# Moving twenty reciprocals of an RWKV-7 / gated-MLP kernel from the vector engine to powers on GpSimd

## The chip, the cores and the metric

The kernel runs on one core of a Trainium2 chip. A core has five engines that each work through their own instruction queue in order: TensorE (PE, matrix products and transposes, with a separate row PEld for its weight loads), VectorE (DVE), ScalarE (ACT), GpSimd (POOL) and SyncE (SP), which here only issues DMAs. The engines wait for each other through semaphores. The metric is the device time of one execution in microseconds. The kernel before has a median of 783.92 us (two runs, 782.73 and 785.11).

## The reference

Two computations follow each other, all in float32. The first is a recurrence over 768 steps for 4 batches times 8 heads with a 40x40 state each, the second a feed-forward block over the 3072 resulting tokens:

```python
for t in range(S):                                   # S = 768, state is D x D, D = 40
    y[:, :, t] = einsum('bhd,bhde->bhe', rt, state)
    Sa = einsum('bhde,bhe->bhd', state, at)
    state_decay = state * wt[:, :, None, :] - einsum('bhd,bhe->bhde', Sa, bt)
    state = state_decay + einsum('bhd,bhe->bhde', vt, kt)
x = y.transpose(0, 2, 1, 3).reshape(B * S, H * D)    # 3072 x 320
h = x @ w_in                                         # 320 x 2048
out = (h * cos(h)) @ w_out                           # 2048 x 320
```

The decay `w` lies between 0.85 and 0.95. The MLP weights arrive as float64.

## The kernel before, in words

The recurrence is cut into **24 units** (`NU`): a unit is a chunk of 64 time steps (`C`) of two of the four batches, all eight heads, laid out as 128 partitions (2 batches x 64 steps) by 8 x 40 elements. Units 2c and 2c+1 hold the two batch pairs of chunk c. Within a chunk the running product W of the decays is needed, because the chunk form of the recurrence works with a·W, b/W and k/W. For units 0 to 3 the running product is scanned on DVE and transposed back through PSUM (`wn`); from unit 4 on it is computed earlier for a whole quarter of the sequence (`ws_scan`, `ws_join`, `ws_down`, `ws_store`), written to DRAM (`wd`), and loaded into the buffer `nat["w", u]`, in SBUF. "The decay" below is this running product.

`over_w(u, wn)` makes `rw` = 1/W (128x320) with one `nc.vector.reciprocal` (L399) and `bn` = b·rw on GpSimd (L400). `p2_kn` (L653) later makes `kn` = k·rw on GpSimd and copies v (L654). The consumers are these: `p1_b` ("pb") turns the `bn` of two units on PE (L364, tile `bT`), `p1_n` ("pn") multiplies bT with aT, and a triangular system per unit is inverted on DVE in many small steps (`inv_step`, `pair_step`, L530 and L534: a multiplication and a subtraction with both inputs in SBUF). `p2_k` turns `kn` (tile `kT`), `p2_g`, `ch_t`, `ch_q`, `ch_ag`, `ch_xa`, `ch_s`, `ch_z` are the chain of matrix products that carries the state from unit u to unit u+2. In `ch_z` GpSimd multiplies the new state by the last decay (`qz`, L802) and the output by W (`yt`, L817), after DVE has added them up (L801, L812). `tokens` and `back` send `yt` through DRAM to make the tokens of the MLP.

The MLP runs in **pieces** (`M` in the plan): `first_a` and `first_b` make `ph` = x·w_in, ACT and DVE form the cosine of it (`turns`) and the product (`gT`, L910), and `second` accumulates `po` = gT·w_out. The float64 weights are rounded to float32 in parts (`rounded`): DMA of the words, then DVE (L265, L269, L275, L281), ACT (L264, L272) and GpSimd (L284) in turn; each part needs the one buffer that an earlier part has left. The first `M` pieces stand among this.

**The order of everything is written out by hand**, in the string `PLAN`: every token issues one step on its engines, and each engine executes its own instructions in that order. `rw4` ... `rw23` are the calls of `over_w` from unit 4 on; `pw`, `pa`, `pb`, `pn` prepare a pair of units; `i` is one step of the inversion, `c` one of the weight rounding, `r` one of the cosine, `^` a matrix product without use that keeps PE running; `L..` are loads. `nat["w", u]` has two buffers, so the load of W for unit u+2 (L144 on SP) waits until `rw` of unit u has been made. `rw` has five buffers, `bn` seven.

Of the kernel before, what the change touches and what calls it, by code (L numbers as in the profile page):

```python
# [12 lines left out]
ALU = mybir.AluOpType  # L13
# [7 lines left out]
def kernel(  # L21
# [12 lines left out]
    nc = tc.nc  # L34
    B, H, S, D = r.shape
    P, C, DP = 128, 64, 64
# [27 lines left out]
    def kept(name, shape, n=1, fill=None, part=lambda t: t, on=nc.gpsimd):  # L64

        tiles = []
        for i in range(n):
            t = const.tile(shape, F32, tag=f"{name}{i}", name=f"{name}{i}")
            if fill is not None:
                on.memset(part(t), fill)  # L70
            tiles.append(t)
        return tiles
# [17 lines left out]
    w_out_sb = const.tile([P, NF, DM], F32, tag="w_out", name="w_out_sb")  # L90
    ident = kept("ident", [P, P])[0]
    make_identity(nc, ident)
    half_pi = kept("half_pi", [P, 1], 1, math.pi / 2, on=nc.vector)[0]
    warm = kept("warm", [P, 1])[0]
    nc.scalar.activation(warm, half_pi, ACTF.Sin)
# [6 lines left out]
    for n, fill in (("w", 1.0), ("a", 0.0), ("b", 0.0)):  # L102
        for i in range(4):
            x = slice((i - 2) * H * DP, (i - 1) * H * DP)
# [291 lines left out]

    def over_w(u, wn):
        rw = ring5.tile([P, H, D], F32, tag="rw", name="rw")
        nc.vector.reciprocal(rw, wn)  # L399
        nc.gpsimd.tensor_tensor(unpad(bn_b[u % 7]), unpad(nat["b", u]), rw, ALU.mult)  # L400
        G["rw", u] = rw

# [7 lines left out]
    def p1_a(u):  # L410
        if u >= 4:
            ps = at("aps")
            for i in range(2):
                turned(ps[:, i], nat["a", u + i])
            for i in range(2):
                a_W(u + i, ps[:, i])
            return
        for u in range(u, u + 2):
            wn = one(ps_h, "wn")
            aps = one(ps_o, "aps")  # L420
            for j in range(4):
                nc.tensor.transpose(
                    wn[:, j * P : (j + 1) * P], G["wb", u][:, j * P + 1 : (j + 1) * P + 1], ident
                )
            from_one(u)
            turned(aps, nat["a", u])
            over_w(u, unpad(wn.rearrange("p (h d) -> p h d", h=H)))
            a_W(u, aps)
# [551 lines left out]
    def seg_rw(u):  # L980
        landed("wb", u)
        if u >= 7:
            needs(f"z{u - 7}")
        over_w(u, unpad(nat["w", u]))
# [292 lines left out]
```

## Time and profile before

| | |
|---|---|
| runs, median | 783.92 us (782.73, 785.11) |
| profiled execution, device time | 778.82 us |
| its span, first to last instruction | 776.9 us |
| granted TensorE clock | 0.994 |
| PE busy | 752.7 us (97%) |
| DVE busy | 504.9 us (65%) |
| ACT busy | 416.5 us (54%) |
| POOL busy | 184.0 us (24%) |
| reciprocals on DVE from unit 4 on (L399, `rw<-nat_w`) | 20, 42.8 us, 2142 ns each |

The profile is of one execution. A busy share is a mean over stages; PE's busy time holds the products without use. Times inside the span ("at 211.7 us") count from its start. In rows of groups the columns are line, engine, operation, output <- inputs, partitions x elements, count, then busy time and mean ns of one, then the idle time of the engine just before, with what ended it.

### The profile page before, as it was taken

To read this page: it belongs to the slowest core of one execution; us is meant where nothing else is said; L and a number is where in the kernel's file an instruction comes from. 1 tells how busy PE (TensorE), PEld (TensorE's weight loads), DVE (VectorE), ACT (ScalarE), POOL (GpSimd) and SP (SyncE) were. 2 spreads that over 40 slices of the span, in tenths; PEclk is the share of its full clock that TensorE was granted. 3 is DMA by queue.
4 is the path that set the end of the run, shared out by engine and by line. 5 is a ranking of instruction groups with operands and counts; after the bars stand their busy time and mean duration, and the time that the engine had idled before them with its cause. 6 is when DMAs were issued, how large, how long until landed. Compare 5 with 4: busy or idle time off the path is not lost.

```text
span 776.9 us, 27804 instructions
## 1 busy us (share of the span) xinstructions
PE 752.7 (97%) x12118; PEld 593.5 (76%) x12118; DVE 504.9 (65%) x965; ACT 416.5 (54%) x762; POOL 184.0 (24%) x320
## 2 busy tenths in 40 slices
PE   8999999899999999999999999999999999999995
PEld 6877877677777877777878778787877787777773
DVE  6796889899769965578835677844476743334221
ACT  1354677655484566546475655465644464544432
POOL 5224635411331242120222202340101121201000
PEclk9999999999999999999999999999999999999998
DMA  9553675362334424423411421423022110200100
GB/s 141 113 128 76 151 183 141 94 140 42 59 103 79 88 61 77 112 72 61 83 34 38 96 62 21 87 54 71 3 46 55 34 23 19 56 10 16 33 17 18
DMA packets 180913, 54.36 MB, mean 70 GB/s; under 512 B 156344, under 2 KB 176440, under 8 KB 180792
## 3 DMA queue, kind: packets, MB, share of 16 engines
q1 hardware_dynamic: 173368, 51.43, 30.2%
q10 hardware_dynamic: 7424, 1.15, 1.0%
q8 instruction: 96, 1.57, 0.8%
q14 instruction: 25, 0.20, 0.1%
HBM read 41.68 MB, written 10.81 MB: 68 GB/s over the span
## 4 chain that ended last, share of the span: by engine, by line
PE 78%; DVE 10%; ACT 5%; issue 2%; DMA 2%; SPq 1%; POOL 1%; ACTq 0%; DVEq 0%; POOLq 0%
PE ph L75 24%; PE po L75 23%; PE dps L75 5%; PE x0ps L75 4%; PE beside L75 3%; PE gram L75 3%; PE sps L75 3%; DVE inv L534 2%; PE vT L364 2%; DVE inv_tmp L530 2%; PE nps L75 1%; PE below L75 1%; DMA words<-in_moe_w_in_dram 1%; PE bT L364 1%; PE qps L75 1%
## 5 line engine op out<-in xcount | busy, mean ns | idle before, releaser
L75 PE MATMUL po<-w_out_sb,gT 128*128 128x320 f32 x768 | 220.5, 438 | 0.0
L75 PEld LDWEIGHTS po<-w_out_sb,gT 128*128 128x128 f32 x768 | 141.3, 190 | 56.5 <-issue 2.4
L75 PE MATMUL ph<-xT,w_in_sb 128*128 128x256 f32 x768 | 183.2, 386 | 0.7 <-DVE gT L910 0.7
L75 PEld LDWEIGHTS ph<-xT,w_in_sb 128*128 128x128 f32 x768 | 140.6, 190 | 30.1 <-issue 9.4
L899 ACT ACTIVATE turns<-ph,rnd 128x512 f32<-128x512 f32 x96 | 62.9, 685 | 130.8 <-PE ph L75 129.7
L903 DVE SCALAR_TENSOR_TENSOR turns<-turns,ph 128x512 f32<-128x512 f32 x96 | 63.3, 679 | 79.7 <-ACT turns L899 79.6
L910 DVE TENSOR_TENSOR gT<-ph,turns 128x512 f32<-128x512 f32 x96 | 65.0, 684 | 33.4 <-ACT turns L907 33.1
L802 POOL TENSOR_TENSOR qz<-qz,wc 128x160 f32<-128x160 f32 x44 | 21.0, 480 | 221.2 <-DVE qz L801 220.3
L907 ACT ACTIVATE turns<-turns,half_pi 128x512 f32<-128x512 f32 x96 | 69.3, 722 | 3.1
L906 ACT ACTIVATE turns<-turns 128x512 f32<-128x512 f32 x96 | 60.2, 627 | 14.4 <-DVE turns L903 13.8
L534 DVE TENSOR_TENSOR inv<-inv,inv_tmp 128x31 f32<-128x31 f32 (+15 forms) x155 | 59.5, 384 | 5.3
L530 DVE TENSOR_TENSOR inv_tmp<-u,inv 128x31 f32<-128x31 f32 (+15 forms) x155 | 56.9, 367 | 3.1
L75 PE MATMUL ph<-xT,w_in_tail 64*64 64x256 f32 (+1 forms) x696 | 51.8, 383 | 0.0
L399 DVE RECIPROCAL rw<-nat_w 128x320 f32<-128x320 f32 x20 | 42.8, 2142 | 0.3 <-POOL kn L653 0.3
L817 POOL TENSOR_TENSOR yt<-yt,wb 128x512 f32<-128x512 f32 x24 | 31.2, 1302 | 42.5 <-DVE yt L812 42.4
L753 DVE COPY x<-x0ps 128x416 f32<-128x416 f32 x24 | 14.2, 591 | 38.6 <-ACT x L752 38.4
L721 ACT COPY qz<-qps 40x512 f32<-40x512 f32 x44 | 25.4, 577 | 22.4 <-PE qps L75 22.0
L75 PEld LDWEIGHTS ph<-xT,w_in_tail 64*64 64x64 f32 (+1 forms) x696 | 26.8, 138 | 13.6 <-issue 8.3
L400 POOL TENSOR_TENSOR bn<-nat_b,rw 128x320 f32<-128x320 f32 x22 | 19.3, 878 | 73.3 <-DVE rw L399 71.5
L775 DVE TENSOR_TENSOR sm<-sps,su 128x256 f32<-128x256 f32 x48 | 18.0, 417 | 25.1 <-ACT sm L770 21.4
L688 DVE TENSOR_TENSOR ag<-gram,su 128x512 f32<-128x512 f32 x24 | 16.5, 686 | 21.4 <-PE gram L75 21.3
L653 POOL TENSOR_TENSOR kn<-nat_k,rw 128x320 f32<-128x320 f32 x24 | 22.0, 915 | 31.7 <-PE sT L705 11.2
(181 smaller groups left out, 1178.0 us busy)
## 6 DMA issues: line engine op xcount, KB each, us to landing
rp<-in_r_dram SPq DMA_DIRECT2D x96, 40.0 KB
out_dram<-ot SPq DMA_DIRECT2D x24, 160.0 KB
vp<-in_v_dram SPq DMA_DIRECT2D x92, 40.0 KB
xd<-yt SPq DMA_DIRECT2D x44, 80.0 KB
nat_a<-in_a_dram SPq DMA_DIRECT2D x43, 80.0 KB
nat_k<-in_k_dram SPq DMA_DIRECT2D x42, 80.0 KB
nat_b<-in_b_dram SPq DMA_DIRECT2D x41, 80.0 KB
ws<-in_w_dram SPq DMA_DIRECT2D x5, 640.0 KB
```

Of the source, the lines that this page charges most:

```text
L75: nc.tensor.matmul(o, lhsT=lhsT, rhs=rhs, start=start, stop=stop, skip_group_check=True)
L364: nc.tensor.transpose(ps[:, i * P : (i + 1) * P], x[:, 2 * i : 2 * i + 2].rearrange("p e d -> p (e d)"), ident)
L399: nc.vector.reciprocal(rw, wn)
L530: nc.vector.tensor_tensor(tmp, u[:, j : j + 1, :j].to_broadcast([P, Q - j, j]), x[:, j:, j : j + 1].to_broadcast([P, Q - j, j]), ALU.mult,)
L534: nc.vector.tensor_tensor(x[:, j:, :j], x[:, j:, :j], tmp, ALU.subtract)
L721: nc.scalar.copy(pick(z[rows], 0, (NZ - C, 2), (NZ, 2 * NB), (1, C)), ps[rows, :, : 2 * NB * C].rearrange("p f (i t) -> p f i t", t=C),)
L817: nc.gpsimd.tensor_tensor(yt.rearrange("p j b t -> p (j b) t"), yt.rearrange("p j b t -> p (j b) t"), wx, ALU.mult)
L899: nc.scalar.activation(n, u, ACTF.Identity, bias=rnd, scale=1.0)
L903: nc.vector.scalar_tensor_tensor(ns[e], ns[e], -ROUND, us[e], ALU.add, ALU.subtract)
L906: nc.scalar.activation(n, n, ACTF.Abs)
L907: nc.scalar.activation(n, n, ACTF.Sin, bias=half_pi, scale=-2.0 * math.pi)
L910: nc.vector.tensor_tensor(gT[:, 2 * e : 2 * e + 2].rearrange("p f t -> p (f t)"), us[e], ns[e], ALU.mult)
```

## The change

From unit 4 on `over_w` no longer uses VectorE. GpSimd raises the decay to the power of -1, with a constant tile of -1.0 as the exponent (read 8 times over by a step of zero). For odd units GpSimd first writes the negated decay into `rw`, raises that to the power of -1 in place, and negates the result; so the ten odd units have three GpSimd instructions and the ten even units one. Units 0 to 3, whose decay lies in PSUM, keep the reciprocal. The constant is set once by VectorE at the start.

```diff
@@ -90,6 +90,7 @@
     w_out_sb = const.tile([P, NF, DM], F32, tag="w_out", name="w_out_sb")
     ident = kept("ident", [P, P])[0]
     make_identity(nc, ident)
+    minus = kept("minus", [P, D], 1, -1.0, on=nc.vector)[0]
     half_pi = kept("half_pi", [P, 1], 1, math.pi / 2, on=nc.vector)[0]
     warm = kept("warm", [P, 1])[0]
     nc.scalar.activation(warm, half_pi, ACTF.Sin)
@@ -396,7 +397,16 @@
 
     def over_w(u, wn):
         rw = ring5.tile([P, H, D], F32, tag="rw", name="rw")
-        nc.vector.reciprocal(rw, wn)
+        if u >= 4:
+            x = wn
+            if u % 2:
+                nc.gpsimd.tensor_scalar(rw, wn, -1.0, None, ALU.mult)
+                x = rw
+            nc.gpsimd.tensor_tensor(rw, x, minus.unsqueeze(1).to_broadcast([P, H, D]), ALU.pow)
+            if u % 2:
+                nc.gpsimd.tensor_scalar(rw, rw, -1.0, None, ALU.mult)
+        else:
+            nc.vector.reciprocal(rw, wn)
         nc.gpsimd.tensor_tensor(unpad(bn_b[u % 7]), unpad(nat["b", u]), rw, ALU.mult)
         G["rw", u] = rw
```

The order of all other instructions on every engine stays as it was.

## The prediction

> **What bounds the kernel now.** I read the page's engine shares first, then PE's waits, then the rows that the change touches, and last GpSimd's and PE's instructions in order of time around them.
>
> ```profile
> PE 752.7 (97%) x12118; PEld 593.5 (76%) x12118; DVE 504.9 (65%) x965; ACT 416.5 (54%) x762; POOL 184.0 (24%) x320
> ...
> L399 DVE RECIPROCAL rw<-nat_w 128x320 f32<-128x320 f32 x20 | 42.8, 2142 | 0.3 <-POOL kn L653 0.3
> ...
> L400 POOL TENSOR_TENSOR bn<-nat_b,rw 128x320 f32<-128x320 f32 x22 | 19.3, 878 | 73.3 <-DVE rw L399 71.5
> ```
>
> PE is idle for 776.9 - 752.7 = 24.2 us in all. Its waits on DVE sum to 8.6 us (the longest are 2.2 us for `ws` and 2.0 us for `wb` at the start, neither of which is a reciprocal). So the 42.8 us that DVE loses lie beside PE's work; freeing them can't give more than about 8.6 us (1.1%). GpSimd has 593 us free, but in one place per unit only: the third row says that before `bn` it stands idle for 73.3 us, nearly all of it waiting for the reciprocal. What matters is how long one power takes, against the room at its place.
>
> **What one power costs.** No power stands in the trace. The nearest rows are GpSimd's own:
>
> ```profile
> L653 POOL TENSOR_TENSOR kn<-nat_k,rw 128x320 f32<-128x320 f32 x24 | 22.0, 915 | 31.7 <-PE sT L705 11.2 <-DMA nat_k<-in_k_dram 8.9 <-DMA rp<-in_r_dram 6.8
> ...
> L654 POOL COPY vvm<-vp 128x320 f32<-128x320 f32 x24 | 12.2, 510 | 9.4 <-DMA vp<-in_v_dram 9.4
> ...
> L512 POOL MEMSET inv<- 128x1024 f32 x6 | 5.7, 952 | 0.1
> ...
> L209 POOL MEMSET bn<- 128x192 f32 x7 | 1.5, 258 | 0.1
> ```
>
> The floor is the multiplication with the same operands' shape, 0.88 us (L400). There is no ceiling among the rows. The two memsets give GpSimd's price of one step per element: (952 - 258) / (1024 - 192) = 0.834 ns, 0.267 us for 320 elements. A float power needs a logarithm, a product, an exponential and the treatment of signs. My estimate is some 40 such steps where the steps of several elements don't overlap fully, hence 40 x 0.267 = **10.7 us**, T below. Fifteen steps would give 4 us, 112 steps 30 us; both ends are kept for the range. DVE's reciprocal, itself a longer operation, takes 2.14 us, against 0.68 us for a DVE product of 512 elements, scaled to 320 some 0.43: five times; five times GpSimd's 0.88 us would be 4.4 us. I take the count of steps because no row suggests that GpSimd has a unit for it as DVE has. A negation is priced as the copy, 0.51 us, so 1.0 us per odd unit.
>
> **Units 4 to 7 (90 to 136 us): no room.** They stand among the rounding of the MLP weights. The chain that ended last, in order of time (start, duration, what), goes through GpSimd there:
>
> ```profile
> 101.41 4.18 DMA words<-in_moe_w_in_dram
> 110.63 2.15 DVE rw L399
> 116.83 1.21 POOL w_in_tail L284
> ```
>
> The next GpSimd instructions behind the power are L284 roundings, whose buffers the next words need, and PE's pieces stand behind them. GpSimd's idle times before these four `bn` are 0.84, 1.50, 1.43 and 0 us, 3.8 in all; one reciprocal lies on the chain (2.15). Cost: 4T + 2.0 for two odd units - 3.8 - 2.15 = 4T - 4.0 = 38.8 us.
>
> **Units 8 to 23: the room of a pair.** PE turns the `bn` of two units together, and PE's order is fixed. The room of a pair runs from the end of the GpSimd instruction before the first power to PE's `bT`, less GpSimd's other work in it and the negation. Units 10 and 11, GpSimd first, then PE:
>
> ```profile
> 211.72 0.87 POOL L400 TENSOR_TENSOR bn<-nat_b,rw 128x320 f32<-128x320 f32 x1 [1.46 <-DVE rw L399]
> 212.55 0.87 POOL L653 TENSOR_TENSOR kn<-nat_k,rw 128x320 f32<-128x320 f32 x1
> 213.37 0.45 POOL L654 COPY vvm<-vp 128x320 f32<-128x320 f32 x1
> 213.96 1.02 POOL L802 TENSOR_TENSOR qz<-qz,wc 128x160 f32<-128x160 f32 x2
> 214.94 1.27 POOL L817 TENSOR_TENSOR yt<-yt,wb 128x512 f32<-128x512 f32 x1
> ...
> 216.97 0.87 POOL L400 TENSOR_TENSOR bn<-nat_b,rw 128x320 f32<-128x320 f32 x1
> ```
>
> ```profile
> 221.80 1.04 PE L364 MATMUL bT<-ident,bn 128*128 128x128 f32 x8
> ```
>
> GpSimd is free at 210.26; unit 11's turn starts at 222.24, after four of the eight. That is 12.0 us, less 6.0 of GpSimd work and 1.0: room 5.0. In the same way: units 8/9 196.2 to 211.3, room 12.4; 12/13 257.3 to 271.7, 11.6; 14/15 304.2 to 314.3, 7.4; 18/19 421.6 to 436.6, 11.0. Unit 20 fits before its neighbours; unit 21 has 501.75 to 513.4, room 9.7. For 16/17 (turned at 383.7, powers possible from 330.9 and 358.1) and 22/23 (521.9 to 553.1) everything fits. With 2T = 21.4 the excess is 9.0 + 16.4 + 9.8 + 14.0 + 10.4 + 1.0 = **60.6 us**. PE has no reserve to make it up.
>
> **What GpSimd holds on DVE.** An inverse step has both inputs in SBUF. The step of 255 elements takes 0.42 us; at 249.20 one took 1.38, while GpSimd multiplied `yt`:
>
> ```profile
> 249.20 1.38 DVE L534 TENSOR_TENSOR inv<-inv,inv_tmp 128x255 f32<-128x255 f32 x1
> ```
>
> ```profile
> 248.84 1.45 POOL L817 TENSOR_TENSOR yt<-yt,wb 128x512 f32<-128x512 f32 x1
> ```
>
> DVE operations that read PSUM (L903, L910) keep their 0.68 us beside GpSimd, and so does the 2.14 us reciprocal. A long power will hold DVE from its first inverse step on, and with it `gT` and the state, for which PE waits. Where the pair itself had room: unit 17 from 361.7 to 369.3 (7.6), unit 16 from 336.3 to 341.6 less the freed reciprocal (3.1), unit 20 from 483.5 to 492.4 less it (6.7): **17.4 us**. The Trainium skill, "SBUF — State Buffer", section "SBUF: two separate sides", speaks of an exclusive lock: a GpSimd instruction, and a DVE instruction with two SBUF inputs, block each other for their whole length. By that rule the sum stands; if they only shared the port, it would be 17 us less. The trace agrees with the rule (1.38 against 0.42).
>
> **At no cost:** the constant's memset (0.13 us for a like one) lies before PE's wait for `ident` at 1.7 us; a freed reciprocal lies beside PE. The load of W for unit u+2 now waits for the power, and SP's queue behind it: W lands 1 to 58 us ahead of its use, so it is hidden with up to T of delay in most units; if not, it adds to the same excess.
>
> **Sum:** 38.8 + 60.6 + 17.4 = 116.8, so 778.8 + 117 = 896 against the profiled execution. The median of the runs shown lies 5 us above that, hence **901 us**, +15%.
>
> **Rivals.** (1) *The power runs near the rate of the other GpSimd operations.* Then 4T - 4.0 is about -0.5 us at T = 0.88, every pair fits, and the time stays at 783 us. It decides where 4T - 4 + (2T - 5.0) + (2T - 7.4) passes 15.7 us (2%), at T = 4.0. For it: the estimate by DVE's ratio, 4.4 us, is near this point. Against it: the steps of a power. This is the case that ends "not slower"; faster by 2% it can't be, by the 8.6 us. (2) *The power goes lane by lane or unoverlapped*, T over 30 us. Then all twenty are in series: at 30 us 600 us less rooms of about 100 us (the 4 and 57 us above, with some 8 us for each of the five units that fit), 784 + 500 = 1284, and 20 us more for each us of T. No row speaks against it. (3) *The sign decides*: negative bases take another path. If the odd units cost 4 us and the even ones 10.7, the first four cost 25.5, the pairs 26, the hold 10: 845 us. If they cost 22, about 61 + 136 + 25: 1006 us. The Trainium skill, "GPSIMD Engine Reference", section 3.1, puts data-dependent branching at about 12 cycles per element; no run here shows it. That the powers aren't there is no rival: the built order has 20 powers and 20 negations on GpSimd, and 20 reciprocals fewer on DVE.
>
> **How the numbers follow.** Chances: forecast (T from 4 to 30) 0.66, rival 1 0.15, rival 2 0.15, rival 3 0.04. The likeliest time is 901. The range leaves out T under 1.5 us (4T - 4 = 2 us: 786) and over 30 us (1284, with some hold 1300): 786 to 1300, wide because T is. Two per cent is about what a measurement of this kernel tells from no change. Slower by more than that: 0.66 + 0.15 + 0.04, 0.85; within it: 0.14; faster: 0.01.
>
> **What would show it.** Right: 20 powers of some 10 us on GpSimd, L400 no longer waiting for DVE, PE idle before `bT` some 10 us per pair and in the 90 to 140 us stretch, inverse steps of several us. Wrong: powers under 4 us, with PE still 97% busy; or times that differ between even and odd units.

## The result, and the profile after

The changed kernel takes a median of 1699.98 us (1699.14 to 1700.82), against 783.92 us: **2.169 times** as long, 95% interval 2.154 to 2.183. The forecast was 901 us, slower; the direction held, the time lies far above the range's upper end of 1300 us.

The page of the changed kernel, engine shares, then groups of instructions (busy time and mean ns of one, then the idle time before them and what ended it):

```profile
PE 795.3 (47%) x12118; PEld 624.3 (37%) x12118; DVE 460.6 (27%) x946; ACT 416.4 (25%) x762; POOL 1231.5 (72%) x360
...
L405 POOL TENSOR_TENSOR rw<-nat_w,minus 128x320 f32<-128x320 f32 x10 | 515.0, 51504 | 4.3 <-DMA nat_w<-wd 4.2
L405 POOL TENSOR_TENSOR rw<-rw,minus 128x320 f32<-128x320 f32 x10 | 515.2, 51519 | 0.8
L365 PE MATMUL bT<-ident,bn 128*128 128x128 f32 x96 | 20.9, 372 | 550.7 <-POOL bn L410 503.6
```

One power takes **51.5 us** where 10.7 were estimated; the second row is the odd units with the negated decay, the first the even ones, and the two agree to 15 ns. GpSimd is now busy for 1231.5 us, more than the whole kernel took before. PE, which was idle for 24 us in all, is idle for 1699.1 - 795.3 = 904 us, 503.6 of them before the turns of `bn`, as the prediction placed them. Of the other long waits in the list of PE's waits, 92.2 us (`kn`), 58.5 (the state `qz`) and 50.3 (a rounded weight) name GpSimd too. Three of 47 to 49 us name DVE and one of 33 us a load of W; they too end 5 to 9 us after the end of a power.

GpSimd in order of time around units 8 and 9:

```profile
400.06 51.49 POOL L405 TENSOR_TENSOR rw<-nat_w,minus 128x320 f32<-128x320 f32 x1
451.62 0.86 POOL L410 TENSOR_TENSOR bn<-nat_b,rw 128x320 f32<-128x320 f32 x1
452.45 1.02 POOL L403 TENSOR_SCALAR rw<-nat_w 128x320 f32<-128x320 f32 x1
453.55 51.49 POOL L405 TENSOR_TENSOR rw<-rw,minus 128x320 f32<-128x320 f32 x1
505.12 1.02 POOL L407 TENSOR_SCALAR rw<-rw 128x320 f32<-128x320 f32 x1
506.22 0.86 POOL L410 TENSOR_TENSOR bn<-nat_b,rw 128x320 f32<-128x320 f32 x1
```

A negation takes 1.02 us, twice the copy by which it was priced.

**Where the 922 us are.** I set PE's instructions, one by one, against those of before. There are 19 waits of over 3.5 us, all of them at a place where PE hardly waited before; they add up to 883 us. The stretches of PE work between them became 39 us longer. 883 + 39 = 922, the difference of the spans (1699.1 - 776.9).

The 39 us are the TensorE clock, the share of full speed that PE is granted. PE's instructions that ran while it was granted at half took 94.5 us, the same ones before 52.4; all others together took 2.8 us less than before. Some 3.6 of the 39 us lie ahead of the first power and aren't the change's: half clock was granted for 6.8 us from 40.4 us on, and the run with a product in the power's place, below, has the same from 38.8 us on. The stretch table of the changed kernel (from:to, length, busy time and count per engine in the order PE, PEld, DVE, ACT, POOL, then the granted clock, DMA share and GB/s), first in a wait, then behind it, then 7 us later:

```profile
570.40:620.00 49.60, 0.00 (x0) 0.00 (x0) 0.00 (x0) 0.00 (x0) 49.43 (x4) 0.50 0.03 6
```

```profile
620.00:627.00 7.00, 6.92 (x139) 6.22 (x140) 2.31 (x5) 4.17 (x8) 3.87 (x8) 0.50 0.41 122
627.00:640.00 13.00, 12.76 (x190) 9.46 (x192) 10.11 (x26) 8.58 (x18) 0.00 (x0) 0.98 0.46 78
```

Within 1 to 5 us of a wait's start the granted clock falls to half, and it stays there until some 3 to 7 us behind the wait's end; so most of the waits cost another 2 to 3 us.

### The profile page after: what moved, and what is told of

Read it like the earlier page. It is cut to its first block, busy times and chain, and to the rows that moved or that the text cites. A ratio compares the mean times of both kernels' runs of the same rounds, so it can differ in the third digit from the quotient of the medians.

```text
span 1699.1 us, 27818 instructions
## 1 busy us (share of the span) xinstructions
PE 795.3 (47%) x12118; PEld 624.3 (37%) x12118; DVE 460.6 (27%) x946; ACT 416.4 (25%) x762; POOL 1231.5 (72%) x360
## 4 chain that ended last, share of the span: by engine, by line
POOL 65%; PE 25%; DVE 4%; issue 2%; ACT 2%; DMA 1%; SPq 0%; POOLq 0%; ACTq 0%; DVEq 0%
POOL rw L405 61%; PE ph L75 8%; PE po L75 6%; PE dps L75 2%; PE x0ps L75 1%; PE beside L75 1%; DVE inv L544 1%; DVE inv_tmp L540 1%; PE gram L75 1%; PE nps L75 1%; PE bT L365 1%; PE sps L75 1%; POOL bn L410 1%; PE below L75 1%; POOL rw L403 1%
## 5 line engine op out<-in xcount | busy, mean ns | idle before, releaser
L405 POOL TENSOR_TENSOR rw<-nat_w,minus 128x320 f32<-128x320 f32 x10 | 515.0, 51504 | 4.3 <-DMA nat_w<-wd 4.2
L405 POOL TENSOR_TENSOR rw<-rw,minus 128x320 f32<-128x320 f32 x10 | 515.2, 51519 | 0.8
L365 PE MATMUL bT<-ident,bn 128*128 128x128 f32 x96 | 20.9, 372 | 550.7 <-POOL bn L410 503.6
L365 PEld LDWEIGHTS bT<-ident,bn 128*128 128x128 f32 x96 | 15.6, 193 | 555.6 <-POOL bn L410 506.9
L75 PE MATMUL ph<-xT,w_in_sb 128*128 128x256 f32 x768 | 194.1, 402 | 0.7 <-DVE gT L920 0.7
L75 PEld LDWEIGHTS ph<-xT,w_in_sb 128*128 128x128 f32 x768 | 148.2, 200 | 33.7 <-issue 10.2
L446 ACT COPY bT<-bT 128x512 f32<-128x512 f32 x24 | 12.9, 589 | 524.0 <-PE bT L365 524.0
L415 DVE TENSOR_TENSOR aT<-aps,wb 128x512 f32<-128x512 f32 x24 | 15.3, 674 | 232.6 <-POOL wb L396 149.7
L365 PE MATMUL kT<-ident,kn 128*128 128x128 f32 x96 | 16.5, 300 | 92.5 <-POOL kn L663 92.2
L811 DVE TENSOR_TENSOR qz<-dps,qz 128x160 f32<-128x160 f32 x44 | 13.8, 318 | 152.1 <-PE dps L75 151.9
```

The lines of the kernel that those rows point to most:

```text
L75: nc.tensor.matmul(o, lhsT=lhsT, rhs=rhs, start=start, stop=stop, skip_group_check=True)
L365: nc.tensor.transpose(ps[:, i * P : (i + 1) * P], x[:, 2 * i : 2 * i + 2].rearrange("p e d -> p (e d)"), ident)
L405: nc.gpsimd.tensor_tensor(rw, x, minus.unsqueeze(1).to_broadcast([P, H, D]), ALU.pow)
```

## The experiments

### The power by itself

A kernel of its own with single powers behind each other, each with its result in a tile of its own (abridged; `e_...` are the exponents, `P` is 128):

```diff
+        power("w320", x);  power("w160", x, q=4);  power("w80", x, q=2);  power("w40", x, q=1);  power("w640", x, q=16)
+        power("p64", x, parts=slice(0, 64));  ...  power("p8", x, parts=slice(0, 8));  power("p1", x, parts=slice(0, 1))
+        power("square", x, "two");  power("root", x, "half");  power("same", x, "p1");  power("m33", x, "m3")
+        power("neg", neg);  power("ones", one);  power("zeros", zero)
```

> A kernel of its own that leaves the whole computation out: it loads some of w and runs single GpSimd powers behind each other, on 128 partitions by 320, 160, 80, 40 and 640 elements, on 64, 32, 8 and 1 partitions, with the exponents -1, 2, 0.5, 1 and -3.3, with negative bases, bases of one and of zero, and beside them a GpSimd product and product with a constant of the same size. Theory 1 (a long chain of steps per element, the same for every value): 51.5 us for 320, 25.8, 12.9, 6.5 and 103 us for the other widths, 51.5 us whatever the number of partitions, the exponent or the sign. Theory 2 (values decide): exponents 1 and 2 or bases of one in a few us. Theory 3 (partitions one by one): 8 partitions or 1 much under 51.5 us. Theory 4 (a fixed price per instruction, such as code that is loaded): 40 elements take nearly as long as 320.

Groups of GpSimd instructions in this kernel, shapes kept apart:

```profile
L45 POOL TENSOR_TENSOR o_w<-x,e_m 128x640 f32<-128x640 f32 x1 | 102.6, 102557 | 0.0
...
L45 POOL TENSOR_TENSOR o_ones<-one,e_m 128x320 f32<-128x320 f32 x1 | 51.4, 51440 | 0.0
...
L45 POOL TENSOR_TENSOR o_p<-x,e_m 1x320 f32<-1x320 f32 x1 | 51.4, 51438 | 0.0
L45 POOL TENSOR_TENSOR o_square<-x,e_two 128x320 f32<-128x320 f32 x1 | 51.4, 51438 | 0.0
...
L45 POOL TENSOR_TENSOR o_neg<-neg,e_m 128x320 f32<-128x320 f32 x1 | 51.4, 51438 | 0.0
...
L45 POOL TENSOR_TENSOR o_w<-x,e_m 128x160 f32<-128x160 f32 x1 | 25.9, 25882 | 0.0
...
L45 POOL TENSOR_TENSOR o_w<-x,e_m 128x40 f32<-128x40 f32 x1 | 6.7, 6744 | 0.0
L67 POOL TENSOR_SCALAR o_ts<-x 128x320 f32<-128x320 f32 x1 | 1.0, 1006 | 0.0
L65 POOL TENSOR_TENSOR o_mult<-x,e_m 128x320 f32<-128x320 f32 x1 | 0.8, 847 | 0.0
```

Theory 1 holds in every point. From 40 to 320 elements the time grows by (51.44 - 6.74) / 280 = 0.160 us per element of a partition, with 0.36 us besides. It is the same for 1 and for 128 partitions, so the partitions aren't worked one by one; it is the same for the exponents -1, 2, 0.5, 1 and -3.3 and for bases that are negative, one or zero, so none of these values takes a shorter path. A product of the same size takes 0.85 us: the power is sixty times as dear.

### Does GpSimd hold DVE?

> A kernel of its own that leaves the whole computation out: VectorE runs products of 255 elements with both inputs in SBUF, and copies of 320 elements from SBUF to SBUF, first alone, then beside one GpSimd power, then beside 25 GpSimd products of 320 elements, then beside 25 GpSimd copies. Theory 1 (GpSimd holds these DVE operations only while it moves data, and a power mostly computes): about 0.42 us each alone and beside the power, well over 1 us beside the products. Theory 2 (an instruction holds DVE for its whole length, as the prediction had it): the first DVE product beside the power takes some 50 us or starts after it.

```diff
+        nc.gpsimd.tensor_tensor(o3, x3, e3, ALU.pow)
+        two(60)                      # VectorE, 255 elements, both inputs in SBUF
+        one(20)                      # VectorE copies, SBUF to SBUF
+        join()
+        for _ in range(25):
+            nc.gpsimd.tensor_tensor(o3, x3, e3, ALU.mult)
+        two(40)
+        ...
```

The code is abridged; 25 GpSimd copies with 40 DVE products beside them follow. The group of the two-input products in four stretches of this kernel: alone, beside the power, beside GpSimd's products, beside its copies.

```profile
L43 DVE TENSOR_TENSOR d<-d,x 128x255 f32<-128x255 f32 x20 | 8.5, 424 | 1.6 <-POOL o L53 1.0
```

```profile
L43 DVE TENSOR_TENSOR d<-d,x 128x255 f32<-128x255 f32 x60 | 26.0, 433 | 3.0 <-POOL o L53 1.0
```

```profile
L43 DVE TENSOR_TENSOR d<-d,x 128x255 f32<-128x255 f32 x26 | 24.5, 942 | 1.8 <-POOL o L53 1.0
```

```profile
L43 DVE TENSOR_TENSOR d<-d,x 128x255 f32<-128x255 f32 x26 | 14.2, 547 | 1.8 <-POOL o L53 1.0
```

All sixty run beside the power at 433 ns, against 424 alone. Beside GpSimd's products they take 942 ns, one per product (a little less than the "well over 1 us" that was expected), and beside its copies 547. DVE's copies took 7.18 us for twenty both alone and beside the power. So a GpSimd product or copy slows DVE, and a power, sixty times as long, doesn't: theory 2, and with it the prediction's 17.4 us, falls. The Trainium skill, "SBUF — State Buffer", section "SBUF: two separate sides", says that whichever comes first has the port pair "for the whole instruction"; for the power the measurement says otherwise. That the power spends most of its time computing between reads is how I read it; the run shows only that DVE isn't held.

The changed kernel's own trace says the same. DVE in order of time, while unit 17's power runs from 987.7 to 1039.2:

```profile
992.34 0.41 DVE L540 TENSOR_TENSOR inv_tmp<-u,inv 128x255 f32<-128x255 f32 x1
992.79 0.42 DVE L544 TENSOR_TENSOR inv<-inv,inv_tmp 128x255 f32<-128x255 f32 x1
```

### A product in the power's place

```diff
-            nc.gpsimd.tensor_tensor(rw, x, minus.unsqueeze(1).to_broadcast([P, H, D]), ALU.pow)
+            nc.gpsimd.tensor_tensor(rw, x, minus.unsqueeze(1).to_broadcast([P, H, D]), ALU.mult)
```

> The changed kernel with a product in place of the power, all else the same; it leaves out the twenty reciprocals, so rw is not 1/W. Theory 1 (the time comes from the power's length, and the freed DVE time is worth nothing because PE is the bound): 0.87 us per operation, 780 to 786 us, the kernel before within 0.5%. Rival (moving the step to GpSimd costs in itself, through the longer queue, the negations or the waits): 10 us or more above the kernel before.

783.06 us, 0.998 of the kernel before (0.994 to 1.001). Everything of the change is there but the length: the queue, the negations, the waits on GpSimd instead of DVE, DVE's freed time. None of it shows; DVE's 42.8 us were worth nothing, as PE's row (755.5 us, 97% of the span) lets expect.

### One power

```diff
+        if u == 17:
+            nc.gpsimd.tensor_tensor(rw, wn, minus.unsqueeze(1).to_broadcast([P, H, D]), ALU.pow)
+        else:
+            nc.vector.reciprocal(rw, wn)
```

> The kernel before with one power, that of unit 17, without negations; the other units keep DVE's reciprocal. Its room by the trace of before: GpSimd is free at 358.1 us and the state behind it (the products qz at 371.9, for PE's transposes at 381.5) and PE's bT at 383.7 wait. Theory 1 (the power delays only what waits for it on GpSimd, DVE goes on): 51.5 - 20 = 31 us, 815 us. Theory 2 (DVE's inverse steps from 361.7 on are held as well, and with them gT for PE): 48 us, 832 us. Theory 3 (every power is in series with all else): 835 us and more.

814.4 us, 1.043 times the kernel before (1.036 to 1.049), 30.5 us more than the 783.9 of the same chip: theory 1. The list of PE's waits of this kernel (waiter, releaser, us in total, times, longest) has one long row:

```profile
PE sT L709 <- POOL qz L806: 29.3, 1, 29.3
```

GpSimd works on the power from 357.65 to 409.14, and the state `qz`, which DVE had ready at 371.9, is multiplied at 410. Between 361 and 382 DVE finishes its inversion undisturbed. So of 51.5 us some 22 are the room and 29 are PE's wait, and the wait is one for the state, which stood in GpSimd's queue behind the power. Behind the wait PE ran at half clock for some 5 us of work, which cost it another 2.7 us.

### One head, four heads, ten units

Three kernels shorten or thin out the powers, without negations:

```diff
+            e = minus.unsqueeze(1).to_broadcast([P, 1, D])
+            nc.gpsimd.tensor_tensor(rw[:, :1], wn[:, :1], e, ALU.pow)
+            nc.vector.reciprocal(rw[:, 1:], wn[:, 1:])
```

> The changed kernel with the power for one of the eight heads alone (40 elements per partition, 6.74 us by the powers measured alone) and DVE's reciprocal for the other seven, for every unit from 4 on, without negations. Theory 1 (the sum of the prediction, with the power's true length and nothing held on DVE): units 4 to 7 cost 4 x 6.74 - 3.8 = 23 us; the rooms of the pairs without the negations are 13.4, 6.0, 12.6, 8.4, 12.0 and 10.7, against 13.5 us for two powers: 15 us; so 784 + 38 = 822 us. Theory 2 (no rooms, all powers in series): 20 x 6.74 = 135, 919 us. Theory 3 (all hidden, since GpSimd has 593 us free): 784 us.

> The changed kernel with the power for four of the eight heads (160 elements, 25.9 us) and DVE's reciprocal for the other four, without negations. Theory 1 (20 x T less rooms that stay the same): the rooms of the changed kernel are 20 x 51.5 + 20 for the negations less the 916 us that it lost, 134 us, some 20 us of which its slowed TensorE clock took back, so 150; 784 + 518 - 150 + 20 for the clock = 1172 us. Theory 2 (in series without rooms): 1302 us. Theory 3 (a price per place, whatever the length): near 1700 us.

> The changed kernel with powers for the ten even units alone, DVE's reciprocal for the odd ones, without negations. Theory 1 (a pair has one room, which one power now has to itself): more than half of the loss goes: 784 + 515 - 95 (the rooms of ten places) + 15 for the clock = 1219 us. Theory 2 (each power costs the same 46 us wherever it stands): 784 + 458 = 1242 us. Theory 3 (without rooms): 1299 us.

| powers | us each | expected | measured |
|---|---|---|---|
| 20 of one head | 6.78 | 822 | 825.0 (1.055 times, 1.051 to 1.058) |
| 20 of four heads | 25.9 | 1172 | 1165.0 (one run) |
| 10 of eight heads | 51.5 | 1219 | 1210.7 (one run) |

Each first theory is met within 9 us, each rival missed by 30 us or more. The first row is the prediction's own table of rooms with the true length put in. That the totals are so close is in part luck: against the kernel before, instruction by instruction, PE's waits grew by 29, 347 and 406 us where 38, 368 and 420 were expected, and its work at half clock took 16, 40 and 27 us longer where 0, 20 and 15 were. The third row says that ten powers cost 428 us where twenty cost 916: 30 us less than half. Some 10 of the 30 are negations, of which the changed kernel has 20 us and this one none; the rest fits a power that has a pair's room to itself, but no run separates the two.

### The clock kept up

Products without use were put in PE's queue where it waits, so that the clock isn't lowered:

```diff
         ps = at("bT")
+        fill = {4: (0, 105), 8: (80, 118), 10: (100, 115), 12: (82, 118), 14: (215, 0), 18: (0, 88), 20: (0, 110), 22: (0, 68)}
         for i in range(2):
+            for _ in range(fill.get(u, (0, 0))[i]):
+                mm(ps[:, i, : 2 * P], ident, pick(ident, 0, (0, 2), (1, P)), True)
             turned(ps[:, i], bn_b[(u + i) % 7])
```

> The changed kernel with matrix products without use (0.43 us each at full clock, 68 to 215 of them) put before the turns of bT for which PE waits longest, so that PE works through about nine tenths of those waits. Theory 1 (part of the loss is TensorE's clock, granted at half for some 7 us after each wait): the stretches of PE work that follow those eleven waits took 19.8 us longer than in the kernel before, and become as short as there: 1700 - 20 = 1680 us, although PE has more to do. Theory 2 (they are longer because ACT and DVE start again behind PE): 1700 us. Theory 3 (the products delay the rest): above 1705 us.

1775.1 us: theory 3, by misplacement. Its chain of work that ended last has the products themselves on it (start, duration, what):

```profile
567.10 45.05 PE bT L75 x200
612.58 49.64 PE bT L75 x230
```

At 567 PE had waited for the PSUM tile, not for `bn`; the first row therefore began after the wait instead of in it, and the second followed upon it. Two more sets stood before the wrong unit. The second try mends the three:

```diff
-        fill = {4: (0, 105), 8: (80, 118), 10: (100, 115), ..., 18: (0, 88), ...}
+        fill = {6: (0, 105), 8: (80, 118), 10: (0, 115), ..., 18: (88, 0), ...}
```

> As the kernel with products before the turns, with three of their places mended: those that stood before units 4/5 (where PE doesn't wait) now before unit 7, none before unit 10 (there the products themselves waited, for the PSUM tile), and those before unit 19 now before unit 18. Ten of PE's waits are worked through. Theory 1 (clock): the stretches behind them took 17.8 us longer than before the change, so 1700 - 18 = 1682 us. Theory 2 (the stretches are longer because the other engines start again behind PE): 1700 us. Theory 3 (the products delay the rest): above 1705 us.

> The changed kernel itself, on the same chip, for the comparison with the kernel with products: 1700 us.

With the products 1693.3 us (2.158 times the kernel before, 2.154 to 2.162), the changed kernel beside it 1703.8 (2.170, 2.165 to 2.174): 10.5 us less, though PE runs 2200 matrix passes more. That is the direction of theory 1 and some 60% of its 18 us. Six of the ten waits are filled so that the stretch behind them is again within 0.5 us of its length before the change, 10.1 us shorter in all than in the changed kernel: 42.3 us against 45.0 (and 42.3 before the change) behind the wait at 765 us of the changed kernel's trace, 18.9 against 21.1 (18.9) behind that at 1353. At the wait that ended at 620 the granted clock of the next 12 us is now full:

```profile
615.00:627.00 12.00, 11.35 (x237) 9.29 (x238) 7.57 (x18) 9.67 (x19) 4.11 (x8) 1.00 0.45 105
```

At the other four, which end at 339, 897, 1182 and 1460 us of this kernel's trace, the products ended 2.9 to 4.4 us ahead of the wait's end. There PE again went on at half clock, and the stretches are 0.7 us shorter to 1.1 us longer than in the changed kernel:

```profile
1182.40:1185.80 3.40, 3.38 (x44) 3.04 (x48) 0.00 (x0) 1.07 (x2) 0.00 (x0) 0.50 0.00 0
```

So the stretch is shortened where the clock was kept up and not where it fell, in one run; this speaks against theory 2.

## Why the prediction was wrong, step by step

**The step that failed is the power's length.** "Some 40 such steps" at 0.267 us gave 10.7 us; measured are 51.5, which by the same measure would be 193 steps. The unit was read rightly from the memsets and the count was a guess, and the range's upper end of 30 us, 112 steps, was a guess of the same kind; no run shows of what steps a power is made. With no row that has a transcendental operation on GpSimd, nothing among the rows bounded T from above, and the range should have said so by reaching further: rival 2, "lane by lane or unoverlapped" with T over 30 us, had a chance of 0.15 and has the length that happened. Of its two readings lane by lane is out by the powers on few partitions; unoverlapped was not tested, so why one element takes 0.160 us stays open. Its price, 784 + 500 at 30 us and 20 us more per us of T, gives 784 + 500 + 430 = 1714 us at 51.5, against 1700. That it comes so close is luck in part: it holds 930 us of waits where there were 883, and nothing for the clock, which cost some 36.

**What bounds the kernel:** right. Freed DVE time is worth nothing (783.1 us with the product), and the loss is PE's idle time.

**Units 4 to 7, no room; a pair's room:** right but for some 10 us. The first four waits of PE, 47 to 50 us each, follow each of the first four powers and come to 195 us, against 204 by 4T - 4.0 with the negations' true length. With short powers (6.74 us) these units cost PE some 10 us of waiting where 23 were reckoned, and the pairs 17 where 15 were; that the total still came to 825 us for 822 is the clock's doing, 16 us which the sum didn't have. At 51.5 us the formula of rival 2 takes rooms of about 100 us for all units; the trace gives 20 x 51.5 + 10 x 2.0 - 883 = 167 us, since what waits for the power on GpSimd waits at different points for different units, often later than the turn of `bn`.

**What GpSimd holds on DVE, 17.4 us:** wrong. A short GpSimd instruction that held an inverse step for its length (1.38 us against 0.42) was read as a rule for every length. Sixty DVE products beside a power ran at full speed.

**At no cost:** W's late load shows once, as a 33 us wait of PE for `nat_w` at 951 us; it stands among the 883. The negation was mis-sized, 1.02 us for 0.51, 10 us in all.

**Not in the sum at all:** the clock. PE that waits 29 to 97 us, nineteen times, starts again at half clock; some 36 us of the 922 (the 39, less the 3.6 ahead of the first power).

**Rivals 1 and 3:** the product in the power's place shows what rival 1 would have been, 783 us. Rival 3, the sign, is out: 51,504 against 51,519 ns.

## What to carry to other kernels

Before an operation moves to an engine on which the trace doesn't show it, measure that one operation; an estimate by counting steps was out by a factor of five here, while the rooms read from the trace gave PE's waits to some 10 us for short powers, and for long ones 930 us where there were 883. An engine's idle total (593 us) is no room: what counts is the stretch between the moment at which it can begin and the moment at which the next thing in its own queue is wanted, some 8 us per unit here (167 us for twenty). And where the bound engine has no idle time, relieving another one gains nothing, so that even a power as short as a product would not have paid (783.06 us against 783.94).

## What the runs showed of the hardware that was not expected

A GpSimd power costs 0.160 us per element of a partition, for every value, exponent and number of partitions (1 to 128) that was run. It doesn't slow a DVE operation with two inputs in SBUF (433 against 424 ns), while a GpSimd product (942 ns) or copy (547 ns) does. A GpSimd product with a constant (1.01 us for 320 elements) takes longer than a product of two tensors (0.85 us). TensorE's granted clock fell to 0.50 within 1 to 5 us of the start of PE's long waits and came back 2.8 to 7.4 us behind their ends. The Trainium skill, "TensorE: Matmul & The Clock Gate", Part 1, has full clock after at least one window of about 3.4 us of sustained work, and says that the window runs freely and doesn't start anew with the kernel. The trace fits at least one window and not one alone: the second 3.4 us behind the wait that ended at 620 us were still granted 0.50, and those behind the wait that ended at 1473 us 0.86.
